# Decoding 64-bit weight blocks in pairs in a fused attention and feed-forward kernel on one Trainium2 core

## The chip, the cores and the metric

The kernel runs on one core of a Trainium2 chip. The metric is device time in microseconds (us). The engines are TensorE (PE, with PEld for its weight loads), VectorE (DVE), ScalarE (ACT), GpSimd (POOL) and SyncE (SP); each works through its own queue of instructions in order.

## The reference

Windowed attention with sinks over 4 batches, 8 heads, 768 positions and 64 columns a head, followed by a two-layer feed-forward net over the 3,072 tokens of 512 columns:

```python
keep = is_sink | in_window            # 4 sink keys, a window of 128
scores = np.where(keep, scale * q @ k.T, -1e9)
a = softmax(scores); x = (a @ v)      # heads side by side: 3072 x 512
h = x @ w_in                          # 512 x 2048
g = np.where(h >= 1, h, np.where(h <= -1, 0, (h + 1) ** 2 / 4))
out = g @ w_out                       # 2048 x 512
```

All inputs are 64-bit floats.

## The kernel before, in words

The 64-bit words of the weights arrive as pairs of 32-bit integers. Each of the two weight matrices is cut into 16 blocks of 128 x 512 values, 512 KB each, and the program calls `weights(n)` for n from 0 to 31: even n is a block of `w_in`, odd n one of `w_out`. One call starts the loads of block n and of up to three more (`AHEAD`) where they were not yet started, the first eight (`SYNC`) on SP's DMA queue and the rest on ACT's, and then decodes block n with `decode`. That is three integer instructions on DVE over 512 columns (L147, L148 and L149), which put sign, exponent and upper fraction bits of the value together in a tile of bits, a rounding copy to the high part on ACT (L150), and a subtraction on DVE that leaves the low part (L151). So a block costs four DVE instructions and one ACT instruction. The bits stand in the pool `moe` under the name "o", with two buffers, which the results of the feed-forward net use later. The blocks as loaded and the decoded blocks of `w_out` share the 16 buffers of the pool `wpool` (4 KB in a partition each); decoded `w_in` has its own memory.

The tokens are worked through in eight chunks of 384 (batch and half). While the attention of chunk c runs (`attn_steps`: loads, scores, transposes and the product with v, of ten or eight units of one head each, two units deep), the feed-forward net of chunk c-1 runs between it (`moe_steps`: `stage1` makes 128 columns of h, `stage2` adds them into the output two blocks later). `spread` puts two lists of steps together in proportion to their weights. The first eight calls of `weights` (`WFIRST`) stand between the attention of chunk 0, the other 24 between the steps of the feed-forward net of chunk 0, that is, in chunk 1. PE runs in this order exactly; the order of DVE, ACT, POOL and SP is set ahead of time by a planner that follows the same list, and may take a step earlier where the engine would otherwise be free in its plan. The first 12 units are done in plain 32-bit products, the later ones with split operands (`k_s`, `q_l`), for which POOL makes the low parts (L216, L218), as it does for the first chunk of the net (`gl`, L427).

In chunk 0 one unit goes: scores on PE (L232), a masked reduction on DVE (L236), the exponential on ACT (L239), a sum on POOL (L244), a reciprocal and a scaling on DVE (L245, L259) and two scalings on ACT (L257), then transposes on PE (L312). From unit 24 on, `recheck` loads each weight block once more and checks its lowest bits, with the pool `chk`.

Of the kernel before, what the change touches and what calls it, by code (L numbers as in the profile page):

```python
# [8 lines left out]
F32 = mybir.dt.float32  # L9
F32R = mybir.dt.float32r  # L10
I32 = mybir.dt.int32
U8 = mybir.dt.uint8
AF = mybir.ActivationFunctionType
ALU = mybir.AluOpType

B, H, S, D = 4, 8, 768, 64
DM, DFF = 512, 2048
P = 128
# [5 lines left out]
QK = CT * P + P + CT * KB  # L24
NJ = DFF // P

NATIVE = 12


# [3 lines left out]


CHECK = range(24, 24 + 2 * NJ)
WFIRST = 8
AHEAD = 3
SYNC = 8

LAG = 2  # L40
LEAD = 0.9
# [8 lines left out]
def attn_ffn(ctx, tc, qk, vx, vs, par, w_in, w_out, out):  # L50
    nc = tc.nc
    const = ctx.enter_context(tc.tile_pool(name="const", bufs=1))
    xpool = ctx.enter_context(tc.tile_pool(name="xpool", bufs=1))
    wpool = ctx.enter_context(tc.tile_pool(name="wpool", bufs=NJ))
    moe = ctx.enter_context(tc.tile_pool(name="moe", bufs=2))
    chk = ctx.enter_context(tc.tile_pool(name="chk", bufs=2))
    moe3 = ctx.enter_context(tc.tile_pool(name="moe3", bufs=3))
    ps_a = ctx.enter_context(tc.tile_pool(name="ps_a", bufs=3, space=bass.MemoryType.PSUM))
    ps_h = ctx.enter_context(tc.tile_pool(name="ps_h", bufs=2, space=bass.MemoryType.PSUM))
# [13 lines left out]
    low, high = par_f[:, :, 0], par_f[:, :, 1]  # L73
# [59 lines left out]
        nc.gpsimd.memset(t, 0.0)  # L133


    w_i = [const.tile([P, 2, DM], F32R, name=f"wi{j}") for j in range(NJ)]
    w_o = [None] * NJ
    raw = {}

# [3 lines left out]
    nc.gpsimd.memset(both, -1)  # L143

    def decode(t, w, words):
        low, x = words[:, :, 0], words[:, :, 1]
        nc.vector.tensor_scalar(w, x, 3, 0x3FFFFFFF, op0=ALU.logical_shift_left, op1=ALU.bitwise_and)  # L147
        nc.vector.scalar_tensor_tensor(w, x, -0x40000000, w, op0=ALU.bitwise_and, op1=ALU.bitwise_or)  # L148
        nc.vector.scalar_tensor_tensor(w, low, 29, w, op0=ALU.logical_shift_right, op1=ALU.bitwise_or)  # L149
        nc.scalar.copy(t[:, 0], w.bitcast(F32))  # L150
        nc.vector.tensor_tensor(t[:, 1], w.bitcast(F32), t[:, 0].bitcast(F32), op=ALU.subtract)  # L151

    top = {}

    def weights(n):
        def f():
            j, i = n // 2, n % 2
            for k in range(n, min(n + min(AHEAD, NJ - n // 2 - 1) + 1, 2 * NJ)):
                if k not in raw:
                    raw[k] = wpool.tile([P, 2 * DM], I32, name="w")  # L160
                    (nc.sync if k < SYNC else nc.scalar).dma_start(raw[k], (w_in, w_out)[k % 2][k // 2].bitcast(I32))
            words = raw[n].rearrange("p (c two) -> p c two", two=2)
            if i:
                w_o[j] = wpool.tile([P, 2, DM], F32R, name="w")
            decode((w_i, w_o)[i][j], moe.tile([P, DM], I32, name="o"), words)
        return f


    again = {}

    def recheck(n, u):
        j, i = n // 2, n % 2
        for k in range(n, min(n + 2, 2 * NJ)):
            if k not in again:
                again[k] = chk.tile([P, 2 * DM], I32, name="again")
                nc.gpsimd.tensor_copy(again[k][0:1, 0:1].bitcast(F32), peak[0:1, u, 2:3])
                nc.sync.dma_start(again[k], (w_in, w_out)[k % 2][k // 2].bitcast(I32))
        if not i:
            top[j] = chk.tile([P, 2, DM], U8, name="top")
        nc.scalar.copy(top[j][:, i], again[n].bitcast(U8).rearrange("p (c e) -> p c e", e=8)[:, :, 7])  # L180
        if i:
            nc.vector.tensor_tensor(both, both, top.pop(j).rearrange("p a c -> p (a c)").bitcast(I32),
                                    op=ALU.bitwise_and)
# [5 lines left out]
    fast = ExitStack()  # L189
# [5 lines left out]
    def load(u):  # L195
        b, h, t0 = u
        T = CT * P
        W = (P if t0 else -NSINK) + CT * KB
        if units.index(u) < NATIVE:

# [20 lines left out]
    def scores(u, i):  # L221
# [9 lines left out]
        for j, q in enumerate(qs):  # L231
# [4 lines left out]
        nc.vector.tensor_tensor_reduce(  # L236
            out=p[:, i, lo:260], in0=ps[:, lo:260], in1=m, scale=-0.0625 if units.index(u) < NATIVE else -0.125, scalar=3.0e38,
            op0=ALU.add, op1=ALU.min, accum_out=peak_i)
# [8 lines left out]
        c0 = 0  # L247
        if units.index(u) >= NATIVE:

            c0 = P  # L250
            nc.vector.tensor_tensor(p[:, i0:, KB:260], p[:, i0:, KB:260], p[:, i0:, 0:P], op=ALU.add)
        for i in range(CT):
            lo = KB if t0 + i == 0 else c0
            r = stat[:, CT + i:CT + i + 1]
            eng = NORM[i] if units.index(u) < NATIVE else "v"
            if eng == "a":
                nc.scalar.activation(p[:, i, lo:260], p[:, i, lo:260], AF.Copy, scale=r)  # L257
            else:
# [133 lines left out]
    def attn_steps(n):  # L392
        us = {k: units[n - k] for k in (-1, 0, 1, 2) if 0 <= n - k < len(units)}
        steps = []
        if n == 0:
            steps.append((0.0, lambda: load(us[0])))
        if -1 in us:
            steps.append((0.0, lambda: load(us[-1])))
        if 1 in us:
            steps.append((0.0, lambda: values(us[1])))  # L400
        qk = [(0.43 if n < NATIVE else 0.22, lambda i=i: scores(us[0], i)) for i in range(CT) if 0 in us]
        tp = [(0.43, lambda i=i: transp(us[1], i)) for i in range(2 if n - 1 < NATIVE else 1) if 1 in us]
        pv = [(1.4 if n - 2 < NATIVE else 1.0, lambda: av(us[2]))] if 2 in us else []
        steps += qk + tp + pv
        if n in CHECK:
            steps.append((0.0, lambda: recheck(n - CHECK[0], n)))
        return steps
# [41 lines left out]
    def moe_steps(row0, tail):  # L449

        x = xpool.tile([P, 2, NCT, CT * P], F32R, name="x")
        o_ps, hs = [], {}
        steps = [(0.0, lambda ct=ct: split(x, ct)) for ct in range(NCT)]
        second = tail[:]
        for j in range(NJ):
            if j < LAG:
                steps += second[j * CT:(j + 1) * CT]
            steps += [(0.49, lambda j=j, ct=ct: stage1(x, j, ct, hs, row0)) for ct in range(NCT)]
            if j >= LAG:
                steps += [(0.65, lambda j=j - LAG, tt=tt: stage2(o_ps, hs, j, tt, row0)) for tt in range(CT)]  # L460
        tail[:] = [(0.65, lambda j=j, tt=tt: stage2(o_ps, hs, j, tt, row0)) for j in range(NJ - LAG, NJ)
                   for tt in range(CT)]
        return steps

    def spread(a, b, lead=1.0):

        wa, wb = (sum(w for w, _ in s) for s in (a, b))
        steps, n, da, db = [], 0, 0.0, 0.0
        for step in b:
            while n < len(a) and da * lead * wb <= db * wa:  # L470
                steps.append(a[n])
                da += a[n][0]
                n += 1
            steps.append(step)
            db += step[0]
        return steps + a[n:]

    wsteps = [(1.0, weights(n)) for n in range(2 * NJ)]
    prev = wsteps[:WFIRST]
    n0 = 0  # L480
    tail = []
    for c in range(len(chunks)):
        n1 = min(H * (c + 1), len(units)) + 2
        attn = [step for n in range(n0, n1) for step in attn_steps(n)]
        n0 = n1
        for _, f in spread(attn, prev, LEAD if c else 1.0):
            f()
        b, t0 = chunks[c]
        prev = moe_steps(b * S + t0 * P, tail)
        if c == 0:  # L490
            prev = spread(wsteps[WFIRST:], prev, WLEAD)

# [70 lines left out]
    with tc.If(other_v > 0):  # L563
        with tc.tile_pool(name="gen", bufs=1) as gen:

            for n in range(2 * NJ):
                words = gen.tile([P, DM, 2], I32, name="words")
# [63 lines left out]
```

## Time and profile before

| what | value |
|---|---|
| median of 3 runs | 737.01 us (736.99 to 737.33) |
| the profiled execution | 737.51 us, of which the span of the trace is 735.8 us |
| PE busy | 702.0 us (95%) |
| DVE busy | 547.3 us (74%) |
| ACT busy | 510.4 us (69%) |
| POOL busy | 329.8 us (45%) |
| DMA traffic | 76.27 MB, mean 104 GB/s |

The shares are means over stages that differ: how busy an engine is where the weights are decoded is read from stretches of the span, not from this table. A busy PE is not PE at its peak, since its matmuls overlap. "Granted clock" is the share of TensorE's full clock of 2.4 GHz that it was given; 0.50 is 1.2 GHz.

### The profile page before, as it was taken

How to read it: one execution, taken by the hardware profiler on the slowest of the kernel's cores; microseconds unless marked ns; L12 is line 12 of the kernel's file. 1: busy time of each engine (PE TensorE's matmuls, PEld its weight loads, DVE VectorE, ACT ScalarE, POOL GpSimd, SP SyncE). 2: the span in 40 equal slices, each digit the busy share in tenths (PEclk: the TensorE clock that was granted, in tenths of full speed). 3: DMA queues.
4: the chain of work that ended last, by engine and by line, in shares of the span. 5: the costliest groups of instructions: out<-in, count | busy, mean ns of one | idle time of the engine just before them, and what ended most of it. 6: DMA issues, size and time to landing. Idle time of an engine off the chain costs nothing.

```text
span 735.8 us, 12453 instructions
## 1 busy us (share of the span) xinstructions
PE 702.0 (95%) x3837; PEld 621.4 (84%) x3837; DVE 547.3 (74%) x1424; ACT 510.4 (69%) x1325; POOL 329.8 (45%) x562
## 2 busy tenths in 40 slices
PE   5889898899999999999999999999989999999996
PEld 3558677899999998999979999899979989989995
DVE  8999999857786777878877887778887677842221
ACT  5997767567677867877767877778757766545332
POOL 3113567645452555636555555646556344500000
PEclk9999999999999999999999999999999999999998
DMA  8875542112232434433433443325422220001001
GB/s 288 289 252 195 187 115 82 51 56 89 54 112 60 148 118 119 131 101 120 124 87 111 155 115 112 97 84 155 135 75 57 86 56 28 9 1 44 0 1 47
DMA packets 43494, 76.27 MB, mean 104 GB/s; under 512 B 7580, under 2 KB 28060, under 8 KB 43420
## 3 DMA queue, kind: packets, MB, share of 16 engines
q1 hardware_dynamic: 39964, 62.81, 27.8%
q10 hardware_dynamic: 3456, 12.58, 5.0%
q8 instruction: 32, 0.52, 0.3%
q14 instruction: 42, 0.34, 0.2%
HBM read 69.09 MB, written 6.29 MB: 102 GB/s over the span
## 4 chain that ended last, share of the span: by engine, by line
PE 58%; DVE 19%; ACT 8%; DMA 6%; issue 4%; POOL 3%; SPq 0%; ACTq 0%; POOLq 0%
PE o_ps L435 25%; PE h_ps L416 24%; PE ps_a L378 4%; PE ps_a L232 3%; DVE o L149 2%; DVE p L259 2%; ACT p L239 2%; DVE o L148 2%; DVE k_s L216 2%; DMA r<-qk 2%; DVE g L425 2%; PE ps_a L324 2%; DVE gl L427 1%; DMA r<-vx 1%; DVE p L236 1%
## 5 line engine op out<-in xcount | busy, mean ns | idle before, releaser
L416 PE MATMUL h_ps<-x,wi 128*128 128x384 f32 x1536 | 310.2, 341 | 0.4 <-DVE x L447 0.4
L416 PEld LDWEIGHTS h_ps<-x,wi 128*128 128x128 f32 x1536 | 263.8, 189 | 9.4 <-issue 0.8
L435 PE MATMUL o_ps<-w,gh 128*128 128x512 f32 x768 | 244.6, 399 | 0.0
L435 PE MATMUL o_ps<-w,gl 128*128 128x512 f32 x384 | 151.7, 395 | 0.0
L435 PEld LDWEIGHTS o_ps<-w,gh 128*128 128x128 f32 x768 | 135.2, 190 | 15.4 <-ACT pt L315 0.4
L218 POOL TENSOR_TENSOR q_l<-r,q_h 128x384 fp32r<-128x384 f32 x52 | 54.1, 1040 | 134.0 <-ACT q_h L217 109.5
L239 ACT ACTIVATE p<-p,peak 128x260 f32<-128x260 f32 (+1 forms) x192 | 93.9, 489 | 29.0 <-DVE peak L236 28.1
L425 DVE SCALAR_TENSOR_TENSOR g<-g,h_ps 128x384 f32<-128x384 f32 x128 | 70.2, 548 | 58.8 <-ACT g L424 58.1
L423 ACT ACTIVATE g<-h_ps,half 128x384 f32<-128x384 f32 x128 | 73.8, 577 | 56.2 <-PE h_ps L416 54.0
L426 ACT CAST gh<-g 128x384 fp32r<-128x384 f32 x128 | 65.5, 512 | 60.3 <-DVE g L425 59.2
L427 DVE TENSOR_TENSOR gl<-g,gh 128x384 fp32r<-128x384 f32 x112 | 71.6, 639 | 24.4 <-ACT gh L426 23.4
L435 PEld LDWEIGHTS o_ps<-w,gl 128*128 128x128 f32 x384 | 72.5, 189 | 17.5
L236 DVE CUSTOM_DVE_ANT_0 p<-ps_a,m 128x260 f32<-128x260 f32 (+1 forms) x192 | 74.3, 400 | 15.5 <-PE ps_a L232 14.1
L216 DVE TENSOR_TENSOR k_s<-k_r,k_s 64x524 fp32r<-64x524 f32 (+1 forms) x46 | 47.5, 1032 | 47.7 <-ACT k_s L214 47.6
L232 PE MATMUL ps_a<-k_s,q_h 128*128 128x260 f32 (+1 forms) x228 | 66.1, 329 | 14.0 <-DMA k_s<-qk 4.8
L424 ACT ACTIVATE g<-g 128x384 f32<-128x384 f32 x128 | 67.0, 524 | 2.6
L378 PE MATMUL ps_a<-pt,v_s 128*128 128x256 f32 (+2 forms) x396 | 66.1, 291 | 0.8 <-DVE peak L236 0.7
L336 POOL TENSOR_SCALAR_AFFINE_SELECT pt<-pt 128x384 fp32r<-128x384 f32 (+1 forms) x104 | 54.6, 526 | 25.6 <-DVE pt L329 22.5
L232 PEld LDWEIGHTS ps_a<-k_s,q_h 128*128 128x128 f32 x228 | 42.1, 199 | 28.3 <-issue 11.0
L378 PEld LDWEIGHTS ps_a<-pt,v_s 128*128 128x128 f32 (+1 forms) x396 | 58.2, 181 | 7.8 <-DVE peak L236 2.3
L259 DVE TENSOR_SCALAR p<-p,stat 128x132 f32<-128x132 f32 (+1 forms) x168 | 62.9, 424 | 0.2
L334 POOL TENSOR_SCALAR_AFFINE_SELECT pt<-pt 128x384 fp32r<-128x384 f32 (+1 forms) x104 | 56.6, 544 | 8.1 <-ACT pt L328 3.1
(108 smaller groups left out, 955.2 us busy)
## 6 DMA issues: line engine op xcount, KB each, us to landing
r<-qk SPq DMA_DIRECT2D x52, 192.0 KB
k_r<-qk SPq DMA_DIRECT2D x32, 262.0 KB
again<-w_in SPq DMA_DIRECT2D x16, 512.0 KB
again<-w_out SPq DMA_DIRECT2D x16, 512.0 KB
w<-w_in ACTq DMA_DIRECT2D x12, 512.0 KB
w<-w_out ACTq DMA_DIRECT2D x12, 512.0 KB
out<-o SPq DMA_DIRECT2D x23, 256.0 KB
r<-vx SPq DMA_DIRECT2D x32, 128.0 KB
```

The lines of the kernel that those rows point to most:

```text
L232: nc.tensor.matmul(ps[:, lo:260], lhsT=q[:, i * P:(i + 1) * P], rhs=k_s[:, c0:c0 + 260 - lo], start=(j == 0), stop=(j == len(qs) - 1))
L236: nc.vector.tensor_tensor_reduce(out=p[:, i, lo:260], in0=ps[:, lo:260], in1=m, scale=-0.0625 if units.index(u) < NATIVE else -0.125, scal ...
L239: nc.scalar.activation(p[:, i, lo:260], p[:, i, lo:260], AF.Exp, bias=peak_i, scale=-1.0, accum_out=stat[:, i:i + 1])
L259: (nc.gpsimd if eng == "p" else nc.vector).tensor_scalar(p[:, i, lo:260], p[:, i, lo:260], r, None, op0=ALU.mult)
L378: nc.tensor.matmul(z, lhsT=w, rhs=y, start=(n == 0), stop=(n == len(mms) - 1))
L416: nc.tensor.matmul(h_ps[:, :T], lhsT=w_i[j][:, w, ct * P:(ct + 1) * P], rhs=x[:, y, ct], start=(ct == 0 and n == 0), stop=(ct == NCT - 1 a ...
L423: nc.scalar.activation(g, h_ps[:, :T], AF.Relu, bias=half, scale=0.5)
L424: nc.scalar.activation(g, g, AF.Square)
L425: nc.vector.scalar_tensor_tensor(g, g, 1.0, h_ps[:, :T], op0=ALU.min, op1=ALU.max)
L426: nc.scalar.copy(gh, g)
L427: (nc.gpsimd if row0 == GL_POOL else nc.vector).tensor_tensor(gl, g, gh.bitcast(F32), op=ALU.subtract)
L435: nc.tensor.matmul(o_ps[tt], lhsT=gg[:, tt * P:(tt + 1) * P], rhs=w_o[j][:, w], start=(j == 0 and n == 0), stop=(j == NJ - 1 and n == 2))
```

## The change

A call of `weights` now loads and decodes two neighbouring blocks of one matrix: one DMA of 1 MB, three DVE instructions over 1,024 columns, one ACT copy and one DVE subtraction of the same width. There are 16 calls in place of 32. The order of the blocks becomes w_in 0 and 1, w_out 0 and 1, w_in 2 and 3, and so on. `WFIRST`, `SYNC` go from 8 to 4 and count the same blocks as before; `AHEAD` goes from 3 blocks to 2 pairs, so up to three pairs, 3 MB, are started by the first call in place of four blocks, 2 MB. The pool `wpool` has 8 buffers of 8 KB. The bits get two buffers of their own in a pool `dec` that is closed after chunk 1, and the pool `chk` of the check takes its place. `decode` takes both shapes; the path for unusual inputs at the end, which this input does not take, still calls it with one block.

```diff
+NP = NJ
-WFIRST = 8
-AHEAD = 3
-SYNC = 8
+WFIRST = 4
+AHEAD = 2
+SYNC = 4
...
-    wpool = ctx.enter_context(tc.tile_pool(name="wpool", bufs=NJ))
+    wpool = ctx.enter_context(tc.tile_pool(name="wpool", bufs=NP // 2))
-    chk = ctx.enter_context(tc.tile_pool(name="chk", bufs=2))
...
-    w_i = [const.tile([P, 2, DM], F32R, name=f"wi{j}") for j in range(NJ)]
+    wi2 = [const.tile([P, 2, 2, DM], F32R, name=f"wi{j}") for j in range(NP // 2)]
+    w_i = [wi2[j // 2][:, j % 2] for j in range(NJ)]
...
     def decode(t, w, words):
-        low, x = words[:, :, 0], words[:, :, 1]
+        low, x = words[..., 0], words[..., 1]
+        high, rest = (t[:, :, 0], t[:, :, 1]) if len(t.shape) == 4 else (t[:, 0], t[:, 1])
...
-        nc.scalar.copy(t[:, 0], w.bitcast(F32))
-        nc.vector.tensor_tensor(t[:, 1], w.bitcast(F32), t[:, 0].bitcast(F32), op=ALU.subtract)
+        nc.scalar.copy(high, w.bitcast(F32))
+        nc.vector.tensor_tensor(rest, w.bitcast(F32), high.bitcast(F32), op=ALU.subtract)
...
     def weights(n):
+        def src(k):
+            return (w_in, w_out)[k % 2][k // 2 * 2:k // 2 * 2 + 2].bitcast(I32).rearrange("j p c -> p j c")
+
         def f():
-            j, i = n // 2, n % 2
-            for k in range(n, min(n + min(AHEAD, NJ - n // 2 - 1) + 1, 2 * NJ)):
+            j, i = n // 2 * 2, n % 2
+            for k in range(n, min(n + min(AHEAD, NP // 2 - n // 2 - 1) + 1, NP)):
                 if k not in raw:
-                    raw[k] = wpool.tile([P, 2 * DM], I32, name="w")
-                    (nc.sync if k < SYNC else nc.scalar).dma_start(raw[k], (w_in, w_out)[k % 2][k // 2].bitcast(I32))
-            words = raw[n].rearrange("p (c two) -> p c two", two=2)
+                    raw[k] = wpool.tile([P, 2, 2 * DM], I32, name="w")
+                    (nc.sync if k < SYNC else nc.scalar).dma_start(raw[k], src(k))
+            words = raw[n].rearrange("p j (c two) -> p j c two", two=2)
             if i:
-                w_o[j] = wpool.tile([P, 2, DM], F32R, name="w")
-            decode((w_i, w_o)[i][j], moe.tile([P, DM], I32, name="o"), words)
+                t = wpool.tile([P, 2, 2, DM], F32R, name="w")
+                w_o[j:j + 2] = t[:, 0], t[:, 1]
+            else:
+                t = wi2[n // 2]
+            decode(t, dec.tile([P, 2, DM], I32, name="bits"), words)
...
-    wsteps = [(1.0, weights(n)) for n in range(2 * NJ)]
+    early = ExitStack()
+    dec = early.enter_context(tc.tile_pool(name="dec", bufs=2))
+    wsteps = [(1.0, weights(n)) for n in range(NP)]
...
+        if c == 1:
+            early.close()
+            chk.append(fast.enter_context(tc.tile_pool(name="chk", bufs=2)))
```

## Rows read from the trace of the kernel before

**Rows 1.** The page: busy time and share of each engine.

```profile
PE 702.0 (95%) x3837; PEld 621.4 (84%) x3837; DVE 547.3 (74%) x1424; ACT 510.4 (69%) x1325; POOL 329.8 (45%) x562
```

**Rows 2.** Busy time by stretch: stretch, length, engines, granted clock, DMA share, GB/s.

```profile
8.00:60.00 52.00, 45.03 (x212) 27.80 (x212) 49.91 (x153) 47.22 (x144) 6.60 (x13) 1.00 0.83 286
60.00:131.00 71.00, 61.23 (x315) 51.47 (x313) 70.61 (x139) 48.03 (x123) 44.06 (x49) 0.95 0.43 136
131.00:736.00 605.00, 592.86 (x3307) 540.06 (x3307) 421.49 (x1112) 413.37 (x1057) 274.62 (x473) 0.99 0.27 83
```

**Rows 3.** Timeline of PE: the three long stalls; start, duration, instruction, idle before.

```profile
86.28 0.36 PE L312 MATMUL ps_a<-ident,p 128*128 128x128 f32 x1 [2.81 <-DVE peak L236]
...
112.76 0.55 PE L324 MATMUL ps_a<-ident,p 128*128 128x128 f32 x3 [3.70 <-DVE peak L236]
...
130.99 0.56 PE L232 MATMUL ps_a<-k_s,q_h 128*128 128x260 f32 x1 [3.13 <-DVE xn L384]
```

**Rows 4.** Busy time by stretch: the one behind the last stall.

```profile
130.99:134.00 3.01, 3.01 (x12) 2.64 (x12) 2.56 (x12) 1.59 (x6) 0.61 (x1) 0.50 0.22 63
```

**Rows 5.** Timeline of DVE from 40.5 us: instructions of 128 and 512 columns.

```profile
40.56 0.41 DVE L147 TENSOR_SCALAR o<-w 128x512 int32<-128x512 int32 x1
40.89 0.42 DVE L236 CUSTOM_DVE_ANT_0 p<-ps_a,m 128x260 f32<-128x260 f32 x1
...
41.24 0.28 DVE L259 TENSOR_SCALAR p<-p,stat 128x128 f32<-128x128 f32 x1
41.44 0.42 DVE L236 CUSTOM_DVE_ANT_0 p<-ps_a,m 128x260 f32<-128x260 f32 x1
...
41.79 0.68 DVE L148 SCALAR_TENSOR_TENSOR o<-w,o 128x512 int32<-128x512 int32 x1
42.39 0.68 DVE L151 TENSOR_TENSOR w<-o,w 128x512 fp32r<-128x512 f32 x1
```

**Rows 6.** Groups of DVE by line and shape, 8 to 60 us.

```profile
L149 DVE SCALAR_TENSOR_TENSOR o<-w,o 128x512 int32<-128x512 int32 x16 | 11.1, 691 | 0.0
...
L147 DVE TENSOR_SCALAR o<-w 128x512 int32<-128x512 int32 x17 | 7.1, 420 | 0.7 <-DMA w<-w_in 0.7
L151 DVE TENSOR_TENSOR wi<-o,wi 128x512 fp32r<-128x512 f32 x8 | 5.5, 684 | 0.5 <-ACT wi L150 0.5
```

**Rows 7.** The same groups of DVE, 60 to 131 us.

```profile
L149 DVE SCALAR_TENSOR_TENSOR o<-w,o 128x512 int32<-128x512 int32 x16 | 16.4, 1023 | 0.0
L148 DVE SCALAR_TENSOR_TENSOR o<-w,o 128x512 int32<-128x512 int32 x16 | 13.1, 817 | 0.0
L151 DVE TENSOR_TENSOR w<-o,w 128x512 fp32r<-128x512 f32 x9 | 10.1, 1125 | 0.0
L147 DVE TENSOR_SCALAR o<-w 128x512 int32<-128x512 int32 x15 | 8.9, 594 | 0.1
L151 DVE TENSOR_TENSOR wi<-o,wi 128x512 fp32r<-128x512 f32 x8 | 7.4, 924 | 0.0
```

**Rows 8.** Timeline of all engines around 82 us: POOL and DVE at once.

```profile
82.36 1.45 POOL L427 TENSOR_TENSOR gl<-g,gh 128x384 fp32r<-128x384 f32 x1 [2.90 <-PE o_ps L435]
...
82.85 1.50 DVE L149 SCALAR_TENSOR_TENSOR o<-w,o 128x512 int32<-128x512 int32 x1
```

**Rows 9.** Busy time by stretch: two stretches of the start.

```profile
5.00:10.00 5.00, 4.49 (x11) 2.54 (x12) 4.12 (x22) 1.32 (x5) 0.37 (x2) 1.00 0.95 298
10.00:15.00 5.00, 2.98 (x11) 1.96 (x12) 4.93 (x15) 4.12 (x14) 1.17 (x2) 1.00 1.02 383
```

**Rows 10.** Timeline: the first decoding instruction; PE's scores of units 2 and 10.

```profile
8.97 0.43 DVE L147 TENSOR_SCALAR o<-w 128x512 int32<-128x512 int32 x1 [0.66 <-DMA w<-w_in]
...
14.58 2.42 PE L232 MATMUL ps_a<-k_s,q_h 128*128 128x128 f32 x6
...
54.17 0.49 PE L232 MATMUL ps_a<-k_s,q_h 128*128 128x128 f32 x2
```

**Rows 11.** Groups of ACT by line and shape, 0 to 140 us.

```profile
L150 ACT CAST wi<-o 128x512 fp32r<-128x512 f32 x16 | 9.9, 616 | 7.2 <-DVE o L149 7.2
L150 ACT CAST w<-o 128x512 fp32r<-128x512 f32 x16 | 9.8, 615 | 2.5 <-DVE o L149 2.5
```

More of the change, by code (lines that the diff above doesn't have):

```diff
@@ L149, in decode @@
         nc.vector.scalar_tensor_tensor(w, low, 29, w, op0=ALU.logical_shift_right, op1=ALU.bitwise_or)
-        nc.scalar.copy(t[:, 0], w.bitcast(F32))
-        nc.vector.tensor_tensor(t[:, 1], w.bitcast(F32), t[:, 0].bitcast(F32), op=ALU.subtract)
+        nc.scalar.copy(high, w.bitcast(F32))
+        nc.vector.tensor_tensor(rest, w.bitcast(F32), high.bitcast(F32), op=ALU.subtract)
     top = {}
     def weights(n):
+        def src(k):
+            return (w_in, w_out)[k % 2][k // 2 * 2:k // 2 * 2 + 2].bitcast(I32).rearrange("j p c -> p j c")
         def f():
-            j, i = n // 2, n % 2
-            for k in range(n, min(n + min(AHEAD, NJ - n // 2 - 1) + 1, 2 * NJ)):
+            j, i = n // 2 * 2, n % 2
+            for k in range(n, min(n + min(AHEAD, NP // 2 - n // 2 - 1) + 1, NP)):
                 if k not in raw:
-                    raw[k] = wpool.tile([P, 2 * DM], I32, name="w")
-                    (nc.sync if k < SYNC else nc.scalar).dma_start(raw[k], (w_in, w_out)[k % 2][k // 2].bitcast(I32))
-            words = raw[n].rearrange("p (c two) -> p c two", two=2)
+                    raw[k] = wpool.tile([P, 2, 2 * DM], I32, name="w")
+                    (nc.sync if k < SYNC else nc.scalar).dma_start(raw[k], src(k))
+            words = raw[n].rearrange("p j (c two) -> p j c two", two=2)
             if i:
-                w_o[j] = wpool.tile([P, 2, DM], F32R, name="w")
-            decode((w_i, w_o)[i][j], moe.tile([P, DM], I32, name="o"), words)
+                t = wpool.tile([P, 2, 2, DM], F32R, name="w")
[3 more added lines that the diff above has]
+            decode(t, dec.tile([P, 2, DM], I32, name="bits"), words)
         return f
     again = {}
+    chk = []
     def recheck(n, u):
@@ L174, in recheck @@
             if k not in again:
-                again[k] = chk.tile([P, 2 * DM], I32, name="again")
+                again[k] = chk[0].tile([P, 2 * DM], I32, name="again")
                 nc.gpsimd.tensor_copy(again[k][0:1, 0:1].bitcast(F32), peak[0:1, u, 2:3])
@@ L178, in recheck @@
         if not i:
-            top[j] = chk.tile([P, 2, DM], U8, name="top")
+            top[j] = chk[0].tile([P, 2, DM], U8, name="top")
         nc.scalar.copy(top[j][:, i], again[n].bitcast(U8).rearrange("p (c e) -> p c e", e=8)[:, :, 7])
@@ L622 @@
     arrays = {n: np.ascontiguousarray(a) for n, a in arrays.items()}
-    nc = bacc.Bacc("TRN2", target_bir_lowering=False, num_devices=1, dynamic_dma_scratch_size=1024)
+    nc = bacc.Bacc("TRN2", target_bir_lowering=False, num_devices=1, dynamic_dma_scratch_size=512)
     aps = [nc.dram_tensor(n, a.shape, mybir.dt.from_np(a.dtype), kind="ExternalInput").ap() for n, a in arrays.items()]
```

## The prediction

> **What bounds the kernel now.** I read the page first: PE is busy 95% of the span and every other engine less than 75% [rows 1], which would make this a kernel bound by PE, on which cheaper decoding is worth nothing. The stretches tell another story, and they were read second. From 8 to 60 us DVE is busy 49.91 of 52 us, from 60 to 131 us 70.61 of 71 us, and after that only 421 of 605 us [rows 2]. The decoding of the weights lies in the first two stretches (32 instructions of L149, 16 in each [rows 6, 7]), so DVE has no room just where the change works. Third, the timeline of PE shows what this costs: in the second stretch PE stands still for 2.81, 3.70 and 3.13 us, and each time a DVE instruction of the attention lets it go on, L236 twice and L384 once [rows 3]. None of the three waits is for a decoded weight: decoding runs ahead of its use, and what PE misses is attention work that stands behind decoding in DVE's queue. Together that is 9.6 us of idle PE. After a stall the granted clock falls as well, 0.50 (1.2 GHz) in the 3.01 us behind the last one [rows 4].
>
> So until about 131 us DVE sets the pace, and after that PE does (592.86 of 605 us busy [rows 2]). PE's later work hangs on PE's own order, so I take it that a microsecond less on DVE before 131 us comes out whole at the end.
>
> **What is removed: 64 DVE instructions.** Sixteen pairs save four DVE instructions each. What is saved is the part of an instruction that does not go with its columns. A duration is not that price, because DVE starts the next instruction before the last one is out: L148 lasts 0.68 us, but L151 starts 0.60 us after it. L259 over 128 columns lasts 0.28 us and the next starts after 0.20 us [rows 5]. From start to start, 384 more columns cost 0.40 us, or 1.04 ns each, and what is left at 128 columns is 0.20 - 0.133 = 0.067 us. An instruction of 1,024 columns should take 0.067 + 1.066 = 1.133 us in place of 2 x 0.60. L147 runs at nearly twice the rate (0.33 us from start to start [rows 5]); I give it the same fixed part. 64 x 0.067 = 4.3 us, 2.3 of them before 60 us (17 of the 32 L147) and 2.0 after [rows 6, 7]. Bounds: nothing, if the two halves of a strided tile cost what two instructions cost; and 64 x (0.28 - 0.133) = 9.4 us, if the whole fixed part of the duration went away. I take 4.3, since rows 5 show start and next start of the very instructions.
>
> The Trainium skill, "VectorE: DVE Perf Modes", section "The TRN2 errata", gives the fixed term of a DVE instruction over SBUF as about 150 cycles in measurement, at 0.96 GHz; 64 of them would be an estimated 10.0 us. The same skill's "Perfetto Trace Analysis", section "Optimizing Scalar/DVE Operations", puts the engine's own share at about 60 ns and says that the other half overlaps with the next instruction; that agrees with the 0.067 us here.
>
> **What stays: the collisions with POOL.** The same L149 lasts 691 ns before 60 us and 1,023 ns after it; L149 at 82.85 us lasts 1.50 us, next to a POOL subtraction that runs from 82.36 for 1.45 us [rows 6 to 8]. Against 691, 684, 684, 420 and 684 ns (L148 priced like L151), the five groups of the second stretch lose 16 x 0.332 + 16 x 0.133 + 9 x 0.441 + 15 x 0.174 + 8 x 0.240 = 15.9 us [rows 6, 7]. POOL's instructions are not touched, and each of them can hold DVE up once, whatever the width of the instruction that it meets. So I leave the 15.9 us as they are; the bounds are no change and half of it, 8.0 us, if the loss goes by DVE instruction.
>
> **What is added at the start.** The first pair can be decoded when 1 MB has landed and not 512 KB. DVE already waits 0.66 us for the first block, until 8.97 us [rows 10]; the other 0.52 MB take 1.4 to 1.8 us at 383 to 298 GB/s [rows 9]. DVE has some attention work of units 0 and 1 in that time: I take 1.2 us lost, between 0 and 1.8. Then the first call puts three pairs on SP's queue, 3.15 MB in place of 2.10 MB, ahead of the q, k and v of unit 2. These come later by 1.05 MB, or 2.7 to 3.5 us at those rates, and PE starts unit 2 at 14.58 us without a wait [rows 10]. For DVE this need not be lost: a pair is 0.60 + 3 x 1.133 = 4.0 us of decoding, and two pairs have landed by then. I take 0.6 us, between 0 and 3.1.
>
> **What moves without a price.** ACT does 16 wide copies in place of 32; the copies now wait 9.7 us in sum for L149 and not the other way round [rows 11], so what ACT saves is covered by DVE's queue. If DVE were no bound, ACT would be near one itself before 60 us (47.22 of 52 us [rows 2]), and the saving there would count, so this can only help. The number of bits buffers stays two, of twice the size. The closing of their pool and the new place of the check's pool come when decoding is long done. The later pairs are loaded through ACT's queue in 12 DMAs in place of 24. The last pair's load starts when the pair before it is decoded, as the last block's does now; it has twice the bytes, and its product is used only in chunk 2. The planner makes a new order for DVE, ACT, POOL and SP; I have no price for it, and it widens the range both ways.
>
> **The sum.** 4.3 - 1.2 - 0.6 = 2.5 us off the profiled execution, 737.51 us (a span of 735.8 and 1.7 around it), gives 735.0 us. The median of the runs is 0.5 us below that execution, so the forecast for it is 734.5 us, 0.34% faster.
>
> **The rivals.**
> *Slower: longer instructions in the way of chunk 0.* From 14.58 to 54.17 us PE works eight units, 4.95 us each [rows 10], and in each of them the attention passes DVE in L236 and again in L245. An instruction that has begun isn't broken off, so a wide one can hold each of these up by 1.133 - 0.60 = 0.53 us more, and ACT's wide copy can do the same there. For it: DVE and ACT are both nearly full there, and the chain of a unit has little slack. Against it: DVE does decoding in the meantime, and that is missing from the second stretch. It decides from 0.31 us a unit on, where it has eaten the 2.5 us, if nothing is paid back later. One full meeting on DVE and a fifth of one on ACT, 0.63 us a unit, cost 8 x 0.63 = 5.0 us: 739.5 us. The Trainium skill, "Perfetto Trace Analysis", section "Optimizing Scalar/DVE Operations", says that where these engines aren't saturated but make bubbles on others, breaking instructions up may help; with DVE at 96% in rows 2 the condition of that sentence is only just not met.
>
> *No change: the first stretch gives nothing back.* If DVE's 2.3 us before 60 us are not the bound there, because units are paced by their chain, 2.0 us remain, and 1.8 us of the start go against it: 736.8 us. For it speaks that DVE is not quite full there, 49.91 of 52 us [rows 2]; against it that what is decoded early is not left for later.
>
> *Much faster.* Either the whole fixed part of the duration is saved, 9.4 - 1.8 = 7.6 us (729.4 us), or the collisions go by DVE instruction, 8.0 + 2.5 = 10.5 us (726.5 us). Rows 5 speak against the first; POOL's unchanged work against the second. Shorter stalls that no longer bring the clock down would add up to 1.5 us behind each (half speed for 3.01 us [rows 4]).
>
> **How the numbers follow.** The forecast case has 0.45, no change 0.17, slower 0.23, much faster 0.15 (0.08 and 0.07). What a measurement of this kernel can tell from no change is about 0.2%, 1.5 us. Faster is then 0.45 + 0.15 = 0.60, the same 0.17, slower 0.23. The forecast's own range is 732.5 to 735.5 us. For 8 times in 10 it is 729.4 to 739.0 us: below are the collisions, 0.07, and above about half of the slower case, 0.12.
>
> **What would show it.** Right: L148, L149 and L151 over 1,024 columns with a next start 1.13 us later in the first stretch; DVE still full, but until about 128 us; the three stalls shorter by some 2 to 3 us in sum; the first L147 near 10.5 us; the same spacing of steps after 140 us. Wrong: a unit of chunk 0 that takes more than 5.2 us; a mean of L149 after 60 us that isn't near 691 x 1.7 + 332 = 1,500 ns; PE stalls that end with a DMA; or new stalls after 140 us, which would come from the planner's new order and not from decoding.

## The result and the profile after

The changed kernel takes 740.9 us (median of 6 runs, 739.28 to 743.43) where the kernel before takes 736.44 us beside it (6 runs): a ratio of 1.0067 [1.0043, 1.0091], 0.7% slower. The forecast was 734.5 us, 0.34% faster. The profiled execution of after took 741.25 us, with a span of 739.5 us.

The page of after, the line of busy times ([rows 1] of before):

```profile
PE 703.0 (95%) x3837; PEld 621.8 (84%) x3837; DVE 531.0 (72%) x1360; ACT 509.5 (69%) x1309; POOL 326.9 (44%) x562
```

DVE has lost exactly the 64 instructions and 16.3 us of busy time, far more than the forecast 4.3 us, and the kernel is slower all the same. The stretches say where it happened. Busy time of after in the three stretches of [rows 2], with the same columns:

```profile
8.00:60.00 52.00, 37.30 (x152) 21.77 (x151) 49.02 (x109) 39.18 (x109) 7.08 (x10) 0.97 0.86 317
60.00:131.00 71.00, 66.10 (x341) 54.33 (x340) 54.22 (x112) 49.85 (x128) 34.49 (x41) 0.95 0.35 106
131.00:736.00 605.00, 596.70 (x3341) 543.69 (x3339) 422.49 (x1118) 418.74 (x1073) 280.77 (x483) 1.00 0.28 84
```

Before 60 us PE does 7.7 us less work than in [rows 2] (37.30 for 45.03) with DVE as full as it was. From 60 to 131 us DVE is no longer full, 54.22 of 71 us in place of 70.61. The counts below show that decoding has moved from the second stretch into the first.

The stretches are cut better by the work. I take the first masked reduction on DVE of a unit (L236 before, L248 after) as the mark of that unit; unit 2 is the first whose loads stand behind the raw weights on SP's queue, unit 10 opens chunk 1, unit 18 chunk 2. By these marks before reaches unit 2, 10 and 18 at 16.8, 55.7 and 154.7 us, after at 20.4, 70.5 and 160.2 us. The span is then this sum: start +3.6 us, chunk 0 from unit 2 on +11.1 (38.97 to 50.11), chunk 1 -9.3 (98.98 to 89.69), all that follows -1.8: together +3.7 us before rounding, as the spans say (735.8 to 739.5).

Busy time of before between the marks, chunk 0 from unit 2 on and chunk 1:

```profile
16.80:55.70 38.90, 34.53 (x172) 20.77 (x172) 37.54 (x116) 36.80 (x114) 4.99 (x10) 1.00 0.83 276
...
55.70:154.70 99.00, 88.86 (x459) 76.42 (x459) 89.56 (x198) 67.21 (x175) 57.73 (x72) 0.95 0.37 118
```

The same of after:

```profile
20.40:70.50 50.10, 39.39 (x169) 23.20 (x169) 49.68 (x104) 40.22 (x110) 7.48 (x10) 0.93 0.80 284
...
70.50:160.20 89.70, 85.60 (x462) 74.13 (x461) 62.64 (x149) 62.62 (x164) 50.96 (x73) 0.98 0.26 76
```

In after DVE works 49.68 of chunk 0's 50.10 us: it sets the pace there. In before it had 1.4 us to spare and ACT 2.1. In chunk 1 DVE's work fell by 26.9 us (89.56 to 62.64) and the stage became only 9.3 us shorter, because PE is then busy 85.60 of 89.70 us. The waits turned round with it: in this stage DVE waited for PE's scores once before and seven times after (total us, times, longest; first before, then after):

```profile
DVE p L236 <- PE ps_a L232: 0.3, 1, 0.3
```

```profile
DVE p L248 <- PE ps_a L244: 6.5, 7, 3.5
```

What DVE does in chunk 0 is in its groups. Before, 16.8 to 55.7 us, the decoding (line, engine, operation, shape, count, busy us, mean ns):

```profile
L149 DVE SCALAR_TENSOR_TENSOR o<-w,o 128x512 int32<-128x512 int32 x13 | 9.0, 693 | 0.0
L148 DVE SCALAR_TENSOR_TENSOR o<-w,o 128x512 int32<-128x512 int32 x12 | 8.2, 685 | 0.1
L147 DVE TENSOR_SCALAR o<-w 128x512 int32<-128x512 int32 x12 | 5.0, 419 | 0.0
L151 DVE TENSOR_TENSOR wi<-o,wi 128x512 fp32r<-128x512 f32 x6 | 4.1, 685 | 0.5 <-ACT wi L150 0.5
L151 DVE TENSOR_TENSOR w<-o,w 128x512 fp32r<-128x512 f32 x6 | 4.1, 681 | 0.0
```

After, 20.4 to 70.5 us (L151, L152 and L153 are the three integer instructions now, L154 the copy on ACT, L155 the subtraction):

```profile
L152 DVE SCALAR_TENSOR_TENSOR bits<-w,bits 128x1024 int32<-128x1024 int32 x10 | 12.3, 1234 | 0.0
L153 DVE SCALAR_TENSOR_TENSOR bits<-w,bits 128x1024 int32<-128x1024 int32 x9 | 10.9, 1215 | 0.0
L151 DVE TENSOR_SCALAR bits<-w 128x1024 int32<-128x1024 int32 x10 | 7.0, 697 | 0.0
L155 DVE TENSOR_TENSOR wi<-bits,wi 128x1024 fp32r<-128x1024 f32 x5 | 6.1, 1223 | 0.0
L155 DVE TENSOR_TENSOR w<-bits,w 128x1024 fp32r<-128x1024 f32 x5 | 6.1, 1221 | 0.0
```

49 instructions of 512 columns, four to a block, are 12.25 blocks; 39 of 1,024 are 19.5 blocks. So in the same eight units DVE works on 7.25 blocks more. The number of blocks between these two marks, counted like this, is what the experiments below are compared by.

The start, in DVE's timeline of after ([rows 10] of before: first L147 at 8.97 us):

```profile
8.58 0.29 DVE L248 CUSTOM_DVE_ANT_0 p<-ps_a,m 128x128 f32<-128x128 f32 x1
...
11.51 0.69 DVE L151 TENSOR_SCALAR bits<-w 128x1024 int32<-128x1024 int32 x1 [2.64 <-DMA w<-w_in]
12.12 0.42 DVE L248 CUSTOM_DVE_ANT_0 p<-ps_a,m 128x260 f32<-128x260 f32 x1
...
14.22 1.22 DVE L153 SCALAR_TENSOR_TENSOR bits<-w,bits 128x1024 int32<-128x1024 int32 x1
15.35 0.69 DVE L151 TENSOR_SCALAR bits<-w 128x1024 int32<-128x1024 int32 x1
```

The first decoding instruction waits 2.64 us for its 1 MB, and the rest of unit 1's reductions, which stand behind it in DVE's queue, wait with it. The last two rows give the pitch of a wide instruction, 1.13 us. PE's timeline of after:

```profile
13.74 0.45 PE L324 MATMUL ps_a<-ident,p 128*128 128x128 f32 x1 [3.27 <-ACT p L269]
...
18.25 2.50 PE L244 MATMUL ps_a<-k_s,q_h 128*128 128x128 f32 x6 [2.79 <-DMA k_s<-qk]
...
69.43 0.49 PE L244 MATMUL ps_a<-k_s,q_h 128*128 128x128 f32 x2
```

Unit 2's scores begin at 18.25 us, and not at 14.58, and wait for a DMA of k. In SP's timeline that load is issued at 11.51 us (8.97 in before):

```profile
8.02 0.33 SPq L215 DMA_DIRECT2D q_h<-qk  x1
11.51 0.33 SPq L216 DMA_DIRECT2D k_s<-qk  x1
```

It is issued at the very time at which the first pair has landed and DVE starts to decode it, and SP's waits from 0 to 25 us put it down to that landing:

```profile
SPq L216 <- DMA w<-w_in: 3.1, 1, 3.1
```

In before the two also coincide, at 8.97 us. So k is issued 2.5 us later than in before, and unit 2's scores start 3.7 us later. Why SP waits for that landing was not tested.

Unit 10 follows at 69.43 (54.17 before): 51.18 us for eight units, 6.40 us each in place of 4.95.

### The profile page after: what moved, and what is told of

It is laid out like the page before. It is cut to its first block, busy times and chain, and to the rows that moved or that the text cites. A ratio compares the mean times of both kernels' runs of the same rounds, so it can differ in the third digit from the quotient of the medians.

```text
span 739.5 us, 12343 instructions
## 1 busy us (share of the span) xinstructions
PE 703.0 (95%) x3837; PEld 621.8 (84%) x3837; DVE 531.0 (72%) x1360; ACT 509.5 (69%) x1309; POOL 326.9 (44%) x562
## 4 chain that ended last, share of the span: by engine, by line
PE 72%; DVE 11%; ACT 6%; DMA 4%; issue 3%; POOL 2%; SPq 0%; ACTq 0%; POOLq 0%
PE h_ps L428 30%; PE o_ps L447 30%; PE ps_a L390 6%; PE ps_a L244 4%; ACT p L251 2%; PE ps_a L336 2%; DVE p L271 1%; DMA w<-w_in 1%; POOL stat L256 1%; DVE k_s L228 1%; DVE bits L152 1%; DMA again<-w_in 1%; DVE bits L153 1%; DMA r<-qk 1%; DVE g L437 1%
## 5 line engine op out<-in xcount | busy, mean ns | idle before, releaser
L248 DVE CUSTOM_DVE_ANT_0 p<-ps_a,m 128x260 f32<-128x260 f32 (+1 forms) x192 | 74.5, 400 | 24.8 <-PE ps_a L244 23.5
L439 DVE TENSOR_TENSOR gl<-g,gh 128x384 fp32r<-128x384 f32 x112 | 68.2, 609 | 24.4 <-ACT gh L438 23.4
L390 PE MATMUL ps_a<-pt,v_s 128*128 128x256 f32 (+2 forms) x396 | 68.2, 297 | 1.4 <-DVE peak L248 1.1
L256 POOL TENSOR_SCALAR stat<-stat 128x3 f32<-128x3 f32 x64 | 32.7, 511 | 72.4 <-ACT p L251 60.6
L348 POOL TENSOR_SCALAR_AFFINE_SELECT pt<-pt 128x384 fp32r<-128x384 f32 (+1 forms) x104 | 53.8, 519 | 24.0 <-DVE pt L341 21.0
```

What stands on the lines that cost most here:

```text
L248: nc.vector.tensor_tensor_reduce(out=p[:, i, lo:260], in0=ps[:, lo:260], in1=m, scale=-0.0625 if units.index(u) < NATIVE else -0.125, scal ...
L390: nc.tensor.matmul(z, lhsT=w, rhs=y, start=(n == 0), stop=(n == len(mms) - 1))
L439: (nc.gpsimd if row0 == GL_POOL else nc.vector).tensor_tensor(gl, g, gh.bitcast(F32), op=ALU.subtract)
```

## The experiments

My first theory was that the change lets the planner take decoding too far ahead. The tile of bits had two buffers of one block; it now has two buffers of two blocks, so four blocks can be between their first instruction and their subtraction where there were two. DVE is a queue in order, and what is put in early stands in front of chunk 0's attention. The rival was that of the prediction: wide instructions hold the attention up. The start was a third, separate cost. In the table, "blocks" is the decoding on DVE between the marks of units 2 and 10, counted from the trace's groups as above; the marks come from the rows of the reductions; the last two columns are the median of all runs and its ratio to the kernel before on the same chip. All ratios are within 2% of 1; what is called faster or slower here has an interval that leaves 1 out. The expectations count all blocks in the planned order ahead of unit 10, those before unit 2 included (14.8 for before and 23.0 for after), so their counts are larger than the table's. The marks come from one profiled run each, and runs of one kernel differ by up to 7 us: the profiles of first_call_2mb and before_three_bits are of runs of 738.03 and 737.92 us, well under their medians, so stages that differ by 1 to 3 us in this table show little.

| kernel | unit 2, us | blocks | unit 2 to 10, us | unit 10 to 18, us | us | ratio |
|---|---|---|---|---|---|---|
| before | 16.8 | 12.25 | 38.9 | 99.0 | 736.44 | 1 |
| after | 20.4 | 19.5 | 50.1 | 89.7 | 740.9 | 1.0067 [1.0043, 1.0091] |
| before_four_bits | 17.0 | 19.25 | 51.8 | 92.1 | 743.94 | 1.0101 [1.0074, 1.0127] |
| before_three_bits | 16.5 | 17.5 | 49.0 | 91.1 | 740.38 | 1.0051 [1.0031, 1.007] |
| narrow_instr | 20.2 | 20.75 | 57.3 | 89.3 | 748.92 | 1.0159 [1.0136, 1.0181] |
| one_bits_buffer | 19.9 | 13.0 | 41.4 | 96.3 | 736.79 | 0.9996 [0.9977, 1.0015] |
| one_bits_narrow | 20.6 | 12.25 | 39.9 | 97.6 | 738.72 | 1.0038 [1.0018, 1.0057] |
| old_start | 17.5 | 17.25 | 47.2 | 92.8 | 737.7 | 1.001 [0.9996, 1.0025] |
| first_call_2mb | 18.9 | 19.5 | 50.3 | 88.9 | 740.93 | 1.006 [1.004, 1.008] |
| one_bits_old_start | 15.9 | 12.25 | 41.0 | 100.1 | 738.4 | 1.0017 [0.9999, 1.0035] |
| one_bits_old_start_half_tail | 15.8 | 13.25 | 42.0 | 95.8 | 733.98 | 0.9969 [0.9949, 0.9988] |
| old_start_gate | 17.6 | 12.25 | 44.8 | 100.5 | 743.83 | 1.009 [1.0059, 1.0122] |
| short_gate | 16.4 | 12.25 | 44.0 | 99.2 | 739.47 | 1.0035 [1.0014, 1.0057] |
| before_gate | 16.5 | 11.75 | 37.3 | 99.8 | 735.65 | 0.9997 [0.9977, 1.0018] |

**before_four_bits** and **before_three_bits**: the kernel before with nothing of the change but the pool of the bits, with four and three buffers of one block. Two things of the change that go with that pool are in both: the later place of `chk`, and `dynamic_dma_scratch_size` of 512 in place of 1,024, an edit that the section on the change does not show.

```diff
+    dec = early.enter_context(tc.tile_pool(name="dec", bufs=4))   # 3 in before_three_bits
-            decode((w_i, w_o)[i][j], moe.tile([P, DM], I32, name="o"), words)
+            decode((w_i, w_o)[i][j], dec.tile([P, DM], I32, name="bits"), words)
...
+        if c == 1:
+            early.close()
+            chk.append(fast.enter_context(tc.tile_pool(name="chk", bufs=2)))
```

> The kernel before, all loads and instructions single as they were, with a pool of its own for the bits with four buffers of 512 columns (the bytes of the changed kernel's two). DVE's order has 22.0 blocks before unit 10 in place of 14.8. Run-ahead: slower than before, 739 to 744 us, PE at unit 10 later than 62 us, and decoding ended before 110 us. Width and start: no change, 736 to 737 us, since neither is touched.

> The kernel before with three bits buffers of 512 columns in a pool of their own. DVE's order has 20.2 blocks before unit 10, between two buffers (14.8) and four (22.0). Theory 'two bounds' (the eight units from 2 to 10 take the larger of their chain, about 38 us, and of DVE's work, 11.6 us of attention and 2.14 us a block): 17.2 blocks x 2.14 + 11.6 = 48 us from unit 2 to unit 10, against 39.0 before and 51.8 with four buffers; chunk 1 gives some 7 us of it back; 739 to 742 us. If buffers only matter when they are four (or by their place in memory), 736 to 737 us.

This is the run that decides. With the loads, the calls, the start and the widths of before, four buffers give a ratio of 1.0101 and three 1.0051, both as expected of the run-ahead, and the two kernels differ in nothing but that count. Nor can the new place of `chk`, the 512 or the separate pool be the cause: one_bits_buffer and one_bits_narrow below have all three, and hold 13.0 and 12.25 blocks. Busy time of before_four_bits between the marks of units 2 and 10, and the largest group of its decoding there:

```profile
17.00:68.80 51.80, 39.57 (x175) 23.04 (x175) 51.68 (x145) 42.33 (x120) 6.78 (x10) 0.90 0.80 283
```

```profile
L148 DVE SCALAR_TENSOR_TENSOR bits<-w,bits 128x512 int32<-128x512 int32 x20 | 13.5, 676 | 0.0
```

DVE is busy 51.68 of 51.80 us, as in after, with narrow instructions of 676 ns, no longer than before's. Twenty of them stand there where the corresponding line of before (its L149) had thirteen. In before_three_bits the profiled span is only 0.3 us longer than before's, since chunk 1 gives back 7.9 us of chunk 0's 10.1; its 0.5% rests on the timed runs.

**narrow_instr**: the change, but each pair decoded in two halves by instructions of 512 columns.

```diff
-            decode(t, dec.tile([P, 2, DM], I32, name="bits"), words)
+            bits = dec.tile([P, 2, DM], I32, name="bits")
+            for h in range(2):
+                decode(t[:, h], bits[:, h], words[:, h])
```

> The changed kernel with its pair loads, order and two 1,024-column bits buffers, but every decoding instruction over 512 columns again (128 DVE and 32 ACT instructions). In DVE's order as built, 24.5 blocks' worth of decoding stands before unit 10's first reduction (23.0 in the changed kernel, 14.8 before). Theory 'run-ahead' (the doubled bits buffers let the planner put more decoding ahead of chunk 0's attention): as slow as the changed kernel or slower, 740 to 745 us, PE at unit 10 not before 68 us. Theory 'width' (an instruction of 1.13 us holds the attention up): back to about 736 to 738 us. Theory 'start' (late first pair, 3 MB ahead of unit 2): as the changed kernel, about 741 us.

The ratio is 1.0159. If wide instructions in the way of the attention had cost the time, this would have come back to before; it is the slowest kernel of the study, above even the 740 to 745 us that the run-ahead was expected to give. Busy time between its marks:

```profile
20.20:77.50 57.30, 42.54 (x171) 25.32 (x171) 55.19 (x150) 41.90 (x120) 6.65 (x10) 0.82 0.73 258
```

20.75 blocks of narrow instructions take DVE 55.19 us, where 19.5 blocks of wide ones took 49.68 of after. The width is a gain, and the rival's mechanism falls.

**one_bits_buffer** and **one_bits_narrow**: one buffer of two blocks, the same memory as before, with wide and with narrow instructions.

```diff
-    dec = early.enter_context(tc.tile_pool(name="dec", bufs=2))
+    dec = early.enter_context(tc.tile_pool(name="dec", bufs=1))
```

> The changed kernel with one 1,024-column bits buffer in place of two (the bytes that the kernel before used). DVE's order has 15.5 blocks before unit 10. Run-ahead: the loss goes, 733 to 737 us, PE at unit 10 by about 58 us, stalls in chunk 1 come back. Width: stays near 741 us. Start: stays near 741 us, as unit 2 still begins near 18 us.

> Pair loads, one 1,024-column bits buffer, and all instructions over 512 columns. 15.5 blocks before unit 10, as in the version with one buffer and wide instructions (736.8 us). Width alone, at equal order: theory 'the wide instructions save DVE time that counts': slower than that version by 2 to 5 us, 739 to 742 us. Theory 'width holds the attention up': faster than it, under 736 us. If DVE isn't the bound at this order: equal, 736 to 738 us.

With one buffer the order is back to 13.0 and 12.25 blocks and chunk 0 to 41.4 and 39.9 us, and the loss is gone (ratio 0.9996), though unit 2 is still late. Between the two only the width was edited (the planner's order differs a little with it): 736.79 against 738.72 us, 1.9 us for wide instructions. By their ratios, each against the kernel before on its own chip, it is 0.0042 or 3.1 us. The intervals do not overlap, but one profile of each shows no such difference (spans of 736.4 and 736.1 us), so this rests on the timed runs alone, and 738.72 us lies between the two expectations for equality and for a saving. It fits a gain of the idea itself, somewhat under the 4.3 us forecast.

**old_start** and **first_call_2mb**: edits of the start alone. Both let the first call load two pairs in place of three; old_start also loads pair 0 by two DMAs and decodes it in halves.

```diff
-            for k in range(n, min(n + min(AHEAD, NP // 2 - n // 2 - 1) + 1, NP)):
+            for k in range(n, min(n + min(AHEAD if n else 1, NP // 2 - n // 2 - 1) + 1, NP)):
...
+                        for h in range(2):                        # old_start only, for pair 0
+                            nc.sync.dma_start(raw[k][:, h], w_in[h].bitcast(I32))
...
+                for h in range(2):                                # old_start only, for pair 0
+                    decode(t[:, h], bits[:, h], words[:, h])
```

> The changed kernel with the start of before: the first call starts two pairs (2 MB), and the first pair is loaded and decoded in two halves; the rest stays wide with two bits buffers. Unit 2 should begin near 14.6 us in place of 18.3. DVE's order has 20.0 blocks before unit 10. Start: 3.7 us off, 737 us. Run-ahead: part of the loss stays, 738.5 to 740 us. Width: about 740 to 741 us.

> The changed kernel with one edit: the first call starts two pairs (2 MB) in place of three. The blocks in DVE's order before each of the units 0 to 10 are the same as in the changed kernel (23.0 before unit 10). If the third MB ahead of unit 2's loads makes the late start, unit 2 begins near 15 us and the time falls by about 2.5 to 3.5 us, to 737.5 to 738.5 us. If the first pair's own size makes it (DVE waits for 1 MB with the scores of unit 1 behind it), unit 2 stays at 17 us or later and the time at 740 us or more.

In old_start unit 2 is back at 17.5 us and, since the order changes with the start, chunk 0 holds 17.25 blocks: 737.7 us, which can't be told from before (1.001 [0.9996, 1.0025]). In first_call_2mb unit 2 comes at 18.9 us, 1.5 us earlier than in after, chunk 0 and its 19.5 blocks stay, and the time is that of after. Without the third pair beside it the first pair is being decoded from 10.04 us on in place of 11.51, and SP issues unit 2's k at 10.03: the third pair is thus part of the 3.6 us (about 1.5), but moving it out of the first call by itself bought nothing that shows, as was expected if the first pair's own size makes the late start.

So one_bits_buffer and old_start each bring the kernel back to before by itself, and old_start takes out 2.25 blocks as well as the late start. How the 4.5 us of loss are split between run-ahead and start is not shown.

**one_bits_old_start**: both repairs, the one buffer and the start, so the two causes of the theory are taken away at once.

> Both repairs on the changed kernel: one 1,024-column bits buffer, and the start of before (two pairs in the first call, the first pair in two halves). DVE's order has 14.0 blocks before unit 10 (14.8 before). Theory 'two causes' (run-ahead and start each cost about 4 us and hide the saving of the wide instructions): their sum goes, 731 to 734 us, faster than before by 0.3 to 0.7%. Theory 'one cause, seen twice' (each repair alone already brings all there is): 736 to 738 us, no change against before.

That the two repairs add up fell: 738.4 us, ratio 1.0017 [0.9999, 1.0035]. Chunk 0 is nearly back (41.0 us, unit 10 at 56.9 us), but chunk 1 takes 100.1 us. The waits of its DVE, 8 to 140 us (total us, times, longest):

```profile
DVE wi L155 <- ACT wi L154: 5.6, 6, 2.0
DVE w L155 <- ACT w L154: 2.8, 3, 1.5
```

8.4 us of DVE idle: with one buffer, DVE has no other pair to decode while ACT's wide copy is under way, and the subtraction then stands at the head of the queue. In before the same waits came to 0.5 us. The one buffer is not all of it: one_bits_buffer has the same buffer and width, and 3.6 us of these waits.

**one_bits_old_start_half_tail**: one_bits_old_start, with copy and subtraction in two halves; the three integer instructions stay wide.

```diff
+        if len(t.shape) == 4:
+            for h in range(2):
+                nc.scalar.copy(high[:, h], w[:, h].bitcast(F32))
+                nc.vector.tensor_tensor(rest[:, h], w[:, h].bitcast(F32), high[:, h].bitcast(F32), op=ALU.subtract)
+            return
```

> One bits buffer and the start of before; the three integer instructions wide, the ACT copy and the DVE subtraction in two halves each, so that a subtraction waits for half a copy. 15.0 blocks before unit 10. Theory 'the single buffer's chain' (DVE stands 8.4 us before subtractions that wait for ACT's copy, which eats the saving of the wide instructions): those waits fall to under 5 us and the time to 733 to 736.5 us. If that idle time isn't on the path, no change against the version with whole copies, 738 us.

733.98 us, ratio 0.9969 [0.9949, 0.9988]: faster than both kernels, by 0.3% against before and about 1% against after. Its waits of the same kind:

```profile
DVE w L157 <- ACT w L156: 1.0, 2, 0.5
...
DVE wi L160 <- ACT wi L159: 0.5, 1, 0.5
```

They fell from 8.4 to 1.5 us, and chunk 1 from 100.1 to 95.8 us. Against before, the profiled span is 3.8 us shorter (732.0): start -1.0, chunk 0 +3.1, chunk 1 -3.2, and -2.7 behind unit 26, which opens chunk 3. Decoding thus explains about 1 us of it. The rest lies where nothing is decoded: PE's waits of over 0.25 us from 200 us on come to 2.7 us here and to 5.2 us in before, most of them for DVE's `sk`, an attention step; whether the order is better there or this one run was, was not tested. The Trainium skill, "Perfetto Trace Analysis", section "Optimizing Scalar/DVE Operations", says that breaking instructions up may let work be done sooner where ScalarE and VectorE aren't saturated but make bubbles on other engines; here breaking up helped as well, but the 8.4 us of bubbles were on DVE itself.

**old_start_gate, short_gate, before_gate**: another way to throttle, put on old_start in the first two. The loads of pairs 7 to 15 (of pairs 7 and 8 in short_gate) wait for a given unit's row maximum, by a small POOL copy into the tile ahead of the load; the bits keep two buffers of two blocks. before_gate puts the same on before.

```diff
+GATE = {7: 8, 8: 8, 9: 9, 10: 10, 11: 11, 12: 12, 13: 13, 14: 14, 15: 14}   # short_gate: {7: 8, 8: 9}
...
+                    if k in GATE:
+                        nc.gpsimd.tensor_copy(raw[k][0:1, 0, 0:1].bitcast(F32), peak[0:1, GATE[k], 2:3])
```

> The start of before, two bits buffers, and the loads of the pairs from the eighth on (k = 7 to 15) held by a small POOL copy of a score maximum until units 8 to 14 are there, so that decoding can't run ahead whatever the buffers. DVE's order has 15.0 blocks before unit 10, as before. Two causes: 731 to 734 us, as with one buffer, since what counts is how much decoding stands ahead of chunk 0's attention and not the buffers. If the second buffer itself were the harm (its place in memory, for instance), it would stay near 738 us.

> As the gated kernel with the start of before, but only the loads of the eighth and ninth pair are held (until units 8 and 9); the later ones run free. 15.0 blocks before unit 10, 28.0 before unit 13 (25.0 with all pairs held). Two bounds: unit 10 near 62 us as in the gated kernel, chunk 1 shorter than its 100.5 us by 4 to 7 us since decoding ends earlier; 735 to 739 us. If holding loads is harmful in itself (POOL's copy and ACT's queue wait), it stays above 741 us.

> The kernel before with the same hold on the loads of blocks 14 to 31. Its order hardly changes: 14.2 blocks before unit 10 (14.8), 28 before unit 15 (30.8). A control for the hold: within 0.3% of before, 734.5 to 738 us, if the hold itself brings nothing; under 734 us if spreading the decoding of chunk 1 is worth something by itself.

The expectation for old_start_gate fell: 743.83 us. The gate brings the 12.25 blocks of before, and chunk 0 does become shorter than in old_start, but not as short as in before, and chunk 1 takes 100.5 us. Busy time of old_start_gate between its marks:

```profile
17.60:62.40 44.80, 36.54 (x176) 21.80 (x175) 36.99 (x91) 35.83 (x105) 6.55 (x13) 0.96 0.69 236
62.40:162.90 100.50, 89.82 (x455) 76.50 (x456) 83.66 (x164) 66.47 (x168) 61.20 (x78) 0.93 0.34 114
```

DVE is idle 7.8 us in the first row and 16.8 in the second (1.4 and 9.4 us in before). In the first row 2.8 us of it is one wait for a raw pair. The planner knows the POOL copies, so the gate changes the order too (12.25 blocks where old_start has 17.25) and doesn't test late data alone. Two gated pairs cost less than nine (1.0035 [1.0014, 1.0057] against 1.009 [1.0059, 1.0122]), but chunk 1 of short_gate is only 1.3 us shorter than that of old_start_gate where 4 to 7 were expected. On before the gate changes nothing (0.9997). How the gates' loss splits between late data and the new order was not separated.

## Why the prediction was wrong, step by step

**The step that failed** is "I take it that a microsecond less on DVE before 131 us comes out whole at the end". It treats chunk 0 and chunk 1 as one pool of DVE work. They are two stages, each with its own limit. The first ends when the attention of eight units has passed DVE, and decoding put before that point is paid in full once DVE is full: from 12.25 to 17.5, 19.25 and 20.75 narrow blocks, chunk 0 goes 38.9, 49.0, 51.8, 57.3 us. What leaves the second is repaid only until PE is full there: chunk 1 takes 88.9 to 89.7 us in the three kernels with the most decoding in chunk 0 (after, first_call_2mb, narrow_instr), whether 9.5 blocks are left for it or, in narrow_instr, fewer. After has put 7.25 blocks more into chunk 0, paid 11.1 us and got 9.3 back. So of the 6.2 us between the forecast for the span (2.5 us shorter) and the profile (3.7 us longer), 6.2 lie here (1.9 us lost in place of 4.3 gained), 1.8 in the start, and -1.8 in what follows.

A sum shows that little else is needed for chunk 0. By the pitches, a narrow block is 0.33 + 3 x 0.60 = 2.13 us [rows 5] and a wide one (0.60 + 3 x 1.13) / 2 = 2.0 us. Take these off the four full chunks: 51.8 - 19.25 x 2.13 = 10.8, 49.0 - 17.5 x 2.13 = 11.7, 57.3 - 20.75 x 2.13 = 13.1, and for after 50.1 - 19.5 x 2.0 = 11.1 us. About 11 to 13 us are left each time, the attention's own DVE work with a few waits (2.1 us of idle DVE in narrow_instr). Before's 12.25 blocks plus the same are 36.9 to 39.2 us beside 38.9 measured.

**What I listed without a price.** "The number of bits buffers stays two, of twice the size" was the cause of the shift, in plain sight, and "the planner makes a new order" was how it acts. I read a buffer only as storage. It is also a limit on how many blocks can be begun, and so on how far the planned order takes decoding ahead. The dose on before shows it: two, three and four buffers give ratios of 1, 1.0051 and 1.0101, and 12.25, 17.5 and 19.25 blocks; each step costs time, though not in proportion to the blocks.

**The saving of width** was right, in kind and in size for one instruction. The next start came after 1.13 us, as forecast, so a wide instruction saves 2 x 0.60 - 1.13 = 0.07 us against two narrow ones. The Trainium skill, "Perfetto Trace Analysis", section "Optimizing Scalar/DVE Operations", puts the fixed share of a DVE instruction over SBUF at about 60 ns; the trace agrees, with 0.07 us. In whole kernels at about equal order the difference is 1.9 to 3.1 us (one_bits_buffer against one_bits_narrow).

**The collisions with POOL** were to stay as they are, and did not: decoding is over before most of POOL's work in chunk 1. The end of it in DVE's timeline of after:

```profile
96.06 2.04 DVE L152 SCALAR_TENSOR_TENSOR bits<-w,bits 128x1024 int32<-128x1024 int32 x1
...
100.55 1.23 DVE L155 TENSOR_TENSOR w<-bits,w 128x1024 fp32r<-128x1024 f32 x1 [0.65 <-ACT w L154]
```

And its two largest groups, 8 to 140 us:

```profile
L152 DVE SCALAR_TENSOR_TENSOR bits<-w,bits 128x1024 int32<-128x1024 int32 x16 | 21.3, 1330 | 0.1
L153 DVE SCALAR_TENSOR_TENSOR bits<-w,bits 128x1024 int32<-128x1024 int32 x16 | 20.3, 1268 | 0.0
```

Against some 1,220 ns undisturbed they lost 16 x 0.110 + 16 x 0.048 = 2.5 us, where the groups of [rows 7] lost 15.9. The 13.4 us of difference and the 4.3 us of the width, 17.7 us, are about the 16.3 us by which DVE's busy time fell. The collisions were avoided in chunk 1, where PE had become the limit, and there 26.9 us less of DVE's work brought 9.3 us.

**The start** was mis-sized: 1.2 + 0.6 = 1.8 us forecast, 3.6 measured. I had the first L147 near 10.5 us; it started at 11.51, and I had not counted that unit 1's reductions stand behind it, nor that SP would not issue unit 2's k before that pair had landed. Unit 2's scores were late by 3.7 us on PE (18.25 against 14.58), and decoding did not cover that.

**What would show it.** The sign "a unit of chunk 0 that takes more than 5.2 us" came, with 6.40 us. "DVE still full, but until about 128 us" did not: decoding ended at 101.8 us. Of the other signs of being wrong, PE's wait for a DMA came (2.79 us, for k), and the wide L149 (now L153) has a mean of 1,338 ns from 60 to 131 us, not one near 1,500. The three long stalls of [rows 3] are gone, as a shift of decoding out of chunk 1 would do; new ones came at the start (3.27 and 2.79 us).

**The rival "slower"** had the place, DVE's queue in chunk 0, and nearly the time, 739.5 us. That the number came so near is luck: its mechanism, wide instructions in the way, is refuted by narrow_instr and by before_four_bits.

Still open: the stretch behind unit 26, 1.6 us shorter in after, which takes 496.1 to 499.8 us in these kernels by where a few late waits of PE fall; the split of the loss between run-ahead and start; and that of the gates' loss.

## What to carry to other kernels

A change in the size or number of buffers between engines is a change of schedule: work out how many units of work it lets begin, and where in an in-order queue the additional ones will stand. Sum the work of the full engine separately for each stage, with the next engine's limit in each; work moved from a stage costs there what it costs, but repays in the other only down to the next limit. When a wide form is tried, give it the memory of the old one and cut the steps that another engine waits on (here copy and subtraction), as the version at 733.98 us does, which keeps the old start as well.

## What the runs showed of the hardware

A decoding block costs DVE more in chunk 1 than in chunk 0, and it does so beside POOL's work: by the busy time of its groups 58.7 us for 17.25 blocks of before (3.4 us each) from unit 10 on, and 30.4 us for 12.25 blocks (2.5 each) between units 2 and 10; in after 23.9 us for 9.5 blocks (2.5) from unit 10 on, where one L152 still lasted 2.04 us, and 42.4 us for 19.5 blocks (2.2) between units 2 and 10. In the timelines of before from unit 10 on, the five L149 that run beside no POOL instruction last 0.68 us in the mean, as in chunk 0, and the twelve beside one 1.14 us. So the cheapest place for the decoding was the one where it did most harm.

The mean granted clock was lower in chunks 0 in which PE stood still for longer: 0.93 in after (10.7 of 50.1 us idle) and 0.82 in narrow_instr (14.8 of 57.3), against 1.00 in before (4.4 of 38.9). Idle time alone does not decide it: PE of short_gate idled 8.9 of 44.0 us at 1.00. DVE was the full engine in chunk 0 of after, and I could not see a cost of the clock there apart from DVE's.
